# One order table for all operations, and half of the weights' low words scaled on GpSimd

## The chip, the cores and the metric

One core of a Trainium2 chip runs the whole program. The metric is the device time of one execution in microseconds (us). The engines are TensorE (PE in the profile; its weight loads are PEld), VectorE (DVE), ScalarE (ACT), GpSimd (POOL), and SyncE (SP), which issues every DMA here. The engines share nothing but memory and semaphores, and each one executes its own instructions strictly in the order in which they were emitted.

## What is computed

Random-feature attention (8 batches of 8 heads, 576 tokens, head size 64, 128 features) is followed by a two-layer network with GELU on all 4608 tokens, 512 to 2048 to 512:

```python
def phi(x):                                    # 128 features of 64 values
    proj = np.einsum('bhsd,md->bhsm', x, omega)
    h = proj - np.sum(x * x, axis=-1, keepdims=True) / 2.0
    h = h - np.max(h, axis=-1, keepdims=True)
    return np.exp(h) / np.sqrt(m)
q_p, k_p = (phi(q_s), phi(k_s))
kv, z = np.einsum('bhsm,bhsd->bhmd', k_p, v), np.sum(k_p, axis=2)
num = np.einsum('bhsm,bhmd->bhsd', q_p, kv)
den = np.einsum('bhsm,bhm->bhs', q_p, z)[..., None] + 1e-06
x = (num / den)                                # 4608 x 512
h = x @ w_in
out = (0.5 * h * (1.0 + erf(h / sqrt(2)))) @ w_out
```

The two weight matrices arrive as 64-bit words and are put together as 32-bit floats on the core.

## The kernel before

**Units.** Attention is cut into 32 units, each two heads of one batch, called u0 to u31. The units of batch 0 (u0 to u3) and of batch 1 (u4 to u7) take a plain 32-bit path (`unit_plain`, L1093 on): `pair` and `shared` project the keys and queries on PE (L951, L958), `top` finds maxima on DVE (L963), `exp_tiles` (L967) or `shift_tiles` and one large `exps` (L972, L976) follow on ACT, then `kv` (L983), `q_trans` (L1021), `q_copy` (L1025), `num_plain` (L1031), `den` (L1045), `rcp` (L1056 to L1058), `div` (L1086). The units from u8 on take a split path (`split_pre`, `split_post`), in which values are carried as a high and a low part: `x_high` on ACT (L1161) and `x_low` on GpSimd (L1170) before the projections `proj` and `proj_q` (L1178, L1200), and `k_high` on GpSimd (L717 through the helper `mul`) and `k_low` on DVE (L1271) before `kv_split` (L1282).

**Blocks.** The network runs over 13 blocks of tokens (256, 256, ten of 384, 256). Block 0 uses 32-bit weights (L1461, L1487). Blocks 1 to 8 use 16-bit high and low parts: three products for each pair of operands, `mm1` (L1466), `gelu` (L1474), `g_high` on ACT (L1478), `g_low` on DVE (L1482), `mm2` (L1490 to L1492). Blocks 9 to 12 use a scheme with seven products in place of eight (`w_prod` L1679, `w_mm2` L1777 to L1779). A block can begin when the units that hold its tokens are done.

**Weights.** Each matrix comes in eight pieces, w1.0 to w1.7 (the first matrix, `w_in`) and w0.0 to w0.7 (the second). For a piece SP loads the raw words (`w_load`, L783, a ring of two buffers), ACT scales the high words (`w_hi`, L788) and converts the low words (`w_lo`, L793), DVE shifts (`w_shift`, L796), GpSimd adds the two (`w_round`, L802), and the largest magnitude is found by ACT for the first six pieces of `w_in` (`w_abs`, L809) and by DVE for the other ten (`w_max`, L805). When all eight pieces of a matrix have been seen, a short chain (`wchain_a` to `wchain_f`) makes a scale, and `w_high` (ACT, L824) and `w_low` (DVE, L828) split the matrix into 16-bit parts.

**The order.** Every step is entered into a `Planner` as an operation with an engine, a cost in us, what it reads and writes, and the ring that its buffer comes from; there are 4920 of them. `Planner.run` (L472 on) is a list scheduler that runs when the program is built: it keeps a clock for each engine, and whenever an engine is free by the costs, it emits that one of the ready operations whose due time is the earliest. The due times come from tables (`STARTS`, `UDUE`, `OFF` for each kind of operation, `MOVES` for single operations). Nothing of this remains on the chip but the order in which each engine meets its instructions.

Of the kernel before, what the change touches and what calls it, by code (L numbers as in the profile page):

```python
# [42 lines left out]
OFF = dict(b_high=-472.0, b_low=68.87, b_sum=505.92, block_be=-596.75, block_high=154.41, block_low=-26.75,  # L43
           block_out=860.38, block_scales=1087.2, block_spread=159.81, bound_a=-4.4, bound_b=540.98, bound_c=-153.41,
           c_gelu=617.86, c_high=519.15, c_low=-947.47, c_low22=-402.54, c_sum=-84.96, chain_a=-692.49, chain_b=-304.15,
           chain_c=-174.23, chain_d=-251.9, den=-276.91, div=-78.97, exp_tiles=500.86, exps=-740.41, g_high=119.81,
           g_low=32.78, gelu=410.19, identity=-401.63, k_high=-264.32, k_low=-842.67, k_shift=268.78, kv=-450.72,
           kv_a=-401.8, kv_b=-498.62, kv_b2=137.69, kv_c=126.76, kv_d=-532.78, kv_split=83.89, kvz_plain=-357.97,
           load_dup=-500.18, load_om=-454.76, load_two=-550.8, load_v=463.08, load_vst=468.47, mm1=-402.39, mm2=439.26,
           nothing=899.66, num=38.14, num_plain=198.27, p2=-435.32, pair=134.89, proj=-15.78, proj_add=-47.53,  # L50
           proj_lo=-1088.01, proj_q=-453.69, q_back=820.26, q_blocks=-307.52, q_copy=-825.62, q_high=102.71, q_low=-58.21,
           q_max=115.0, q_max2=-738.48, q_max3=-292.57, q_max4=-375.03, q_max5=-248.0, q_max6=852.42, q_shift=29.04,
           q_trans=-350.16, rcp=-489.6, s_high=944.67, s_low=-468.09, s_sum=43.05, s_sum2=-111.06, scale_om=21.42,
           shared=-393.46, shift_tiles=-284.33, split_om=1280.88, store=-902.88, store_dma=1009.48, top=161.02, v_a=122.39,
           v_b=125.44, v_max=354.57, v_scales=208.4, v_spread=-1174.86, w_abs=1352.56, w_hi=-1126.5, w_high=423.95,
           w_lo=217.93, w_load=218.15, w_low=-223.86, w_max=-31.41, w_mm2=-9.77, w_prod=14.23, w_round=665.96,
           w_seed=603.07, w_shift=-118.27, w_snap=969.6, warm=580.57, wchain_a=297.7, wchain_b=-362.6, wchain_c=-875.34,
           wchain_d=1130.76, wchain_e=-246.9, wchain_f=881.58, x_high=-158.88, x_low=-494.15, zeros=-566.36)
# [367 lines left out]
class Planner:  # L426
# [45 lines left out]
    def run(self, lat, hop, alloc, put):  # L472
# [1442 lines left out]
```

## Time and profile before

| | |
|---|---|
| Median of 3 runs | 983.53 us (982.3 to 984.62) |
| Profiled execution: its time, its span | 982.61 us, 980.8 us |
| Granted TensorE clock, mean over the span | 0.991 of full speed |
| PE busy | 954.8 us, 97% of the span |
| PE weight loads busy | 627.2 us, 64% |
| DVE busy | 752.8 us, 77% |
| ACT busy | 763.1 us, 78% |
| POOL busy | 403.2 us, 41% |
| DMA | 71.01 MB, mean 72 GB/s |

The span reaches from the first to the last instruction; 1.8 us of the execution lie around it. A busy share is an average over stages that are unlike: weights and attention fill the first 110 us, attention and network run side by side until about 890 us, and the end is network alone. So the profile is read in stretches. Matmuls overlap, so the busy time of PE counts stretches in which it had work, and its idle time is what is left.

### The profile page before, as it was taken

To read this page: it belongs to the slowest core of one execution; us is meant where nothing else is said; L and a number is where in the kernel's file an instruction comes from. 1 tells how busy PE (TensorE), PEld (TensorE's weight loads), DVE (VectorE), ACT (ScalarE), POOL (GpSimd) and SP (SyncE) were. 2 spreads that over 40 slices of the span, in tenths; PEclk is the share of its full clock that TensorE was granted. 3 is DMA by queue.
4 is the path that set the end of the run, shared out by engine and by line. 5 is a ranking of instruction groups with operands and counts; after the bars stand their busy time and mean duration, and the time that the engine had idled before them with its cause. 6 is when DMAs were issued, how large, how long until landed. Compare 5 with 4: busy or idle time off the path is not lost.

```text
span 980.8 us, 18864 instructions
## 1 busy us (share of the span) xinstructions
PE 954.8 (97%) x6572; PEld 627.2 (64%) x6572; DVE 752.8 (77%) x2007; ACT 763.1 (78%) x1591; POOL 403.2 (41%) x612
## 2 busy tenths in 40 slices
PE   7999999989999999999999999999999999999998
PEld 6666666756555556666655666566657677677676
DVE  3789889998999887989887888989888764662222
ACT  6989778888788887988899788988788765674443
POOL 2443316775658445645552653542574102130000
PEclk7989999999999999999999999999999999999999
DMA  9875114322122123124112221221021000000000
GB/s 277 242 227 192 55 49 138 100 72 57 44 70 69 45 75 94 43 70 132 50 49 84 62 63 57 62 76 58 25 56 52 25 1 34 1 1 34 1 33 23
DMA packets 46286, 71.01 MB, mean 72 GB/s; under 512 B 13680, under 2 KB 22256, under 8 KB 46192
## 3 DMA queue, kind: packets, MB, share of 16 engines
q1 hardware_dynamic: 46192, 69.81, 24.4%
q8 instruction: 52, 0.85, 0.4%
q14 instruction: 42, 0.34, 0.1%
HBM read 60.36 MB, written 9.44 MB: 71 GB/s over the span
## 4 chain that ended last, share of the span: by engine, by line
PE 51%; DVE 10%; ACT 4%; issue 1%; POOL 0%; ACTq 0%; DVEq 0%
PE h L1466 12%; PE at L1679 6%; PE h L1679 5%; PE acc L1490 4%; PE acc L1492 4%; PE acc L1491 4%; PE acc L1778 4%; PE acc L1779 4%; PE acc L1777 4%; PE at L1040 2%; PE at L1282 1%; DVE gl L1482 1%; PE at L1178 1%; PE at L1200 1%; DVE mx L1205 1%
## 5 line engine op out<-in xcount | busy, mean ns | idle before, releaser
L1170 POOL TENSOR_TENSOR r<-xt,r 64x288 fp32r<-64x288 f32 (+2 forms) x216 | 168.8, 798 | 156.7 <-ACT r L1161 122.1
L1466 PE MATMUL h<-xh,wih 128*128 128x384 f16 (+1 forms) x512 | 163.6, 320 | 6.0 <-DVE gl L1482 5.7
L1466 PE MATMUL h<-xh,wil 128*128 128x384 f16 (+1 forms) x512 | 163.7, 320 | 0.0
L1466 PE MATMUL h<-xl,wih 128*128 128x384 f16 (+1 forms) x512 | 163.7, 320 | 0.0
L1490 PE MATMUL acc<-woh,gh 128*128 128x512 f16 x368 | 140.1, 381 | 0.0
L1492 PE MATMUL acc<-wol,gh 128*128 128x512 f16 x368 | 139.5, 379 | 0.0
L1491 PE MATMUL acc<-woh,gl 128*128 128x512 f16 x368 | 139.5, 379 | 0.0
L1466 PEld LDWEIGHTS <-wih 128*128 128x128 f16 x1024 | 97.6, 98 | 56.3 <-issue 0.9
L1161 ACT CAST r<-xt 128x256 fp32r<-128x256 f32 (+2 forms) x216 | 81.4, 407 | 14.7 <-PE at L1178 6.5
L1482 DVE SCALAR_TENSOR_TENSOR gl<-h,bs,gh 128x384 f16<-128x384 f32 (+1 forms) x128 | 75.2, 590 | 16.6 <-ACT gh L1478 15.3
L1474 ACT ACTIVATE h<-h,bs 128x384 f32<-128x384 f32 (+1 forms) x128 | 68.9, 539 | 23.1 <-PE h L1466 21.8
L1478 ACT ACTIVATE gh<-h,bs 128x384 f16<-128x384 f32 (+1 forms) x128 | 72.0, 565 | 16.3 <-PE acc L1492 13.3
L1466 PEld LDWEIGHTS <-wil 128*128 128x128 f16 x512 | 50.0, 98 | 37.8 <-issue 10.1
L1777 PE MATMUL acc<-woh,gh 128*128 128x512 f16 (+1 forms) x192 | 69.4, 362 | 0.0
L1778 PE MATMUL acc<-woh,gl 128*128 128x512 f16 (+1 forms) x192 | 69.4, 361 | 0.1
L1779 PE MATMUL acc<-wol,gh 128*128 128x512 f16 (+1 forms) x192 | 69.4, 361 | 0.0
L1679 PEld LDWEIGHTS <-w 128*128 128x128 f16 x768 | 60.1, 98 | 8.3
L1492 PEld LDWEIGHTS <-gh 128*128 128x128 f16 x368 | 36.0, 98 | 43.4
L1490 PEld LDWEIGHTS <-gh 128*128 128x128 f16 x368 | 35.8, 97 | 30.9
L1051 ACT ACTIVATE dt<-at,vsc 64x288 f32<-64x288 f32 x96 | 47.6, 496 | 7.8 <-PE at L1040 5.5
L1178 PE MATMUL at<-om,r 128*128 128x256 f32 x216 | 51.2, 330 | 2.6 <-POOL r L1170 1.9
L1491 PEld LDWEIGHTS <-gl 128*128 128x128 f16 x368 | 36.1, 98 | 27.3
(291 smaller groups left out, 2510.1 us busy)
## 6 DMA issues: line engine op xcount, KB each, us to landing
xt<-in_qT SPq DMA_DIRECT2D x56, 288.0 KB, 3.8
xt<-in_kT SPq DMA_DIRECT2D x56, 288.0 KB, 3.9
out_x<-o SPq DMA_DIRECT2D x35, 256.0 KB, 2.0
raw<-in_w_in SPq DMA_DIRECT2D x16, 512.0 KB, 6.0
raw<-in_w_out SPq DMA_DIRECT2D x16, 512.0 KB, 4.8
w<-in_v SPq DMA_DIRECT2D x24, 320.0 KB, 3.0
vt<-in_v SPq DMA_DIRECT2D x8, 320.0 KB, 4.3
out_x<-o SPq DMA_DIRECT2D x2, 128.0 KB, 1.7
```

Source lines behind the costliest of these rows:

```text
L1161: nc.scalar.copy(G['r', u, x][:, 0:b - a], xf[:, a:b])
L1170: nc.gpsimd.tensor_tensor(r, xf[D:, a:b], r, op=ALU.subtract)
L1466: nc.tensor.matmul(h[:, 0:t], w, (G['xh', n, j], G['xh', n, j], G['xl', n, j])[k][:, 0:t], start=(i == 0), stop=(i == 3 * NJ - 1))
L1478: nc.scalar.activation(G['gh', n, c][:, 0:t], G['h', n, c][:, 0:t], AF.Copy, scale=G['bs', n][:, 3:4])
L1482: nc.vector.scalar_tensor_tensor(G['gl', n, c][:, 0:t], G['h', n, c][:, 0:t], G['bs', n][:, 3:4], G['gh', n, c][:, 0:t], op0=ALU.mult, op1 ...
L1490: nc.tensor.matmul(acc, gh[:, s], woh[:, c, c0:c1], start=(c == 0), stop=False)
L1491: nc.tensor.matmul(acc, gl[:, s], woh[:, c, c0:c1], start=False, stop=False)
L1492: nc.tensor.matmul(acc, gh[:, s], wol[:, c, c0:c1], start=False, stop=(c == NF - 1))
L1679: nc.tensor.matmul(b[:, g * h:(g + 1) * h], w, x[:, kt], start=first and k == 0, stop=last and k == 6 * GP - 1, skip_group_check=True)
L1777: nc.tensor.matmul(acc, gh, woh[:, c, c0:c1], start=begin, stop=False)
L1778: nc.tensor.matmul(acc, gl, woh[:, c, c0:c1], start=False, stop=False)
L1779: nc.tensor.matmul(acc, gh, wol[:, c, c0:c1], start=False, stop=end)
```

## The change

- `Planner.run` loses the scheduler, its costs, due times and tables. In their place stands `ORDER`, a list of the 4920 operations by number; a letter behind a number says which of the PSUM rings a tile takes. `run` emits them in that order. The graph of operations is the same, so every engine has the same operations as before, but for the eight of the next point; the costs in the calls of `op` are changed here and there, and are no longer used for anything.
- For every other piece of both matrices (w1.0, w1.2, w1.4, w1.6, w0.0, w0.2, w0.4, w0.6) GpSimd converts the low words (`w_lo_p`) and not ACT.
- The scale of the 16-bit key features moves into the exponential: `exps` adds a constant (a per-partition tile `kln`) for the units on the split path, `k_high` multiplies by 1 and `k_low` is a plain subtraction in place of a multiply and subtract.
- Other switches that the diff brings (`px`, `wg`, `kl`) are set so that they change nothing.

The core of the diff, tables cut:

```diff
-KSC = 2.0 ** 15
+KSC = 2.0 ** 11
+KLN = 7.6246189861593985
...
+X = dict(plain=8, kvp=8, eb0=8, ttr=1, pair=0, amax=63, qm=1, xm=0, km=0, prelu=1, n0=9, h=2, at=3, vs=5, wr=('h', 'at'),
+         tx=4, ss=4, xh=8, gh=3, xp=0, qs=0, kl=99, wl=21845, wg=0, px=0)
+ORDER = """
+0 3 6 7 151 42 41 157 4 1 8 43 9bca 14b 2 76 15 12 16 10 152 13 17 154 153 11 18 44aba 20 155 19 49b 45 21 47 50 51 163 77
...
-    def run(self, lat, hop, alloc, put):
...
+    def run(self, alloc, put):
+        done = set()
+        for x in ORDER.split():
+            i = x.rstrip('abc')
+            o, pick = self.ops[int(i)], x[len(i):] or 'a' * 4
+            assert o.deps <= done and o.after <= done
+            for (names, k), z in zip(o.new, pick):
+                name = names if isinstance(names, str) else names['abc'.index(z)]
...
             put(o)
...
+        nc.vector.memset(kln, KLN)
...
+    def w_lo_p(pc):
+        nc.gpsimd.tensor_scalar(pc.l if pc.l is not None else raw(pc)[1], raw(pc)[1].bitcast(U32), 2.0 ** -29, 1.0, op0=ALU.mult, op1=ALU.mult)
...
         op('ACT', 1.08, w_hi, pc, w=[rk + ('hi',)], r=[rk])
-        op('ACT', 1.08, w_lo, pc, r=[rk], w=pc.lk if pc.l is not None else [rk + ('lo',)])
+        on = X['wl'] >> (i + 8 * (1 - win)) & 1
+        op('POOL' if on else 'ACT', 1.5 if on else 1.08, w_lo_p if on else w_lo, pc, r=[rk], w=pc.lk if pc.l is not None else [rk + ('lo',)])
...
-            nc.scalar.activation(u.et, u.et, AF.Exp)
+            nc.scalar.activation(u.et, u.et, AF.Exp, bias=kln if u.split else 0.0)
...
-        mul(nc.gpsimd, kk[:, 0, ts], u.et[:, ts], KSC)
+        mul(nc.gpsimd, kk[:, 0, ts], u.et[:, ts], 1.0)
...
-        nc.vector.scalar_tensor_tensor(kk[:, 1, ts], u.et[:, ts], KSC, kk[:, 0, ts], op0=ALU.mult, op1=ALU.subtract)
+        (nc.gpsimd if u.k >= X['kl'] else nc.vector).tensor_tensor(kk[:, 1, ts], u.et[:, ts], kk[:, 0, ts], op=ALU.subtract)
```

What the table says, read out engine by engine and set beside the order of before (operations of each engine that stand at the same place, the mean shift of all by number of places, the largest shift):

| engine | operations | same place | mean shift | largest |
|---|---|---|---|---|
| PE | 1597 | 493 | 1.7 | 13 |
| ACT | 1375 (1383 before) | 17 | 8.1 | 71 |
| DVE | 1261 | 204 | 3.1 | 88 |
| POOL | 521 (513 before) | 3 | 7.8 | 93 |
| SP | 150 | 77 | 1.0 | 8 |

- PE before: `warm`, `pair(u0,0)`, `pair(u1,0)`, `shared(u0)`, `shared(u1)`, `pair(u0,1)`. After: `pair(u0,0)`, `shared(u0)`, `warm`, `pair(u0,1)`, `pair(u1,0)`, `shared(u1)`. (`warm` is 22 matmuls on zeros; the first two of after are the projection of the keys of u0 and the half tiles that its two heads share.)
- SP before: both loads of u0, then `load_om`. After: `load_om` first.
- ACT before: `exp_tiles` of u0 (four tiles), twice two tiles, `w_hi(w1.0)`, `w_lo(w1.0)`. After: `exp_tiles` of the two shared tiles of u0, `w_hi(w1.0)`, then eight more tiles of u0.
- ACT ahead of `exps(u4)`: the table puts the same operations there as before, less `w_lo` of w1.0, w1.2, w1.4 and w1.6, `w_abs(w1.4)` and `bound_a(u3)`. Ahead of the first `w_high`, `w_lo(w0.0)` is missing too.
- POOL: `w_lo` of a piece stands right ahead of its own `w_round`, but for w0.0.
- The number of changes between the exponential and the GELU on ACT is 56 in both orders.

## Rows read from the trace of the kernel before

**Rows 1.** The page: busy time, share of the span and instructions of each engine.

```profile
PE 954.8 (97%) x6572; PEld 627.2 (64%) x6572; DVE 752.8 (77%) x2007; ACT 763.1 (78%) x1591; POOL 403.2 (41%) x612
```

**Rows 2.** Busy us by stretch: length, PE, PEld, DVE, ACT, POOL, granted clock, DMA share, GB/s.

```profile
0.00:24.00 24.00, 18.06 (x140) 15.29 (x140) 8.84 (x25) 16.36 (x44) 5.40 (x8) 0.79 0.95 275
24.00:48.00 24.00, 21.80 (x203) 16.52 (x201) 18.01 (x47) 23.75 (x61) 9.04 (x7) 1.00 0.88 252
48.00:72.00 24.00, 21.57 (x133) 15.01 (x129) 19.30 (x54) 21.94 (x39) 10.94 (x16) 0.86 0.72 227
72.00:96.00 24.00, 24.00 (x128) 15.72 (x127) 22.83 (x41) 22.39 (x34) 9.85 (x4) 1.00 0.55 175
...
144.00:168.00 24.00, 24.00 (x154) 15.48 (x153) 20.20 (x61) 20.35 (x50) 14.11 (x25) 1.00 0.45 141
168.00:192.00 24.00, 22.85 (x171) 16.29 (x170) 23.43 (x76) 20.99 (x58) 17.30 (x27) 1.00 0.37 98
...
336.00:360.00 24.00, 23.81 (x151) 14.75 (x150) 22.84 (x62) 19.97 (x43) 12.62 (x18) 1.00 0.21 55
...
696.00:720.00 24.00, 21.57 (x120) 12.54 (x119) 20.61 (x62) 18.97 (x46) 19.73 (x37) 1.00 0.18 50
```

**Rows 3.** Waits of PE, whole span: us in total, times, longest us.

```profile
PE h L1466 <- DVE gl L1482: 5.7, 9, 1.6
```

**Rows 4.** Timeline of ACT, 0 to 75 us: start us, duration us, what [idle before].

```profile
8.24 1.14 ACT L967 ACTIVATE et<-at,nm 128x128 f32<-128x128 f32 x4 [6.22 <-DVE nm L963]
...
12.20 1.14 ACT L793 ACTIVATE w<-raw 128x1024 int32<-128x1024 uint32 x1
13.22 1.14 ACT L967 ACTIVATE et<-h,nm 128x128 f32<-128x128 f32 x4
...
50.33 1.08 ACT L809 ACTIVATE w<-w 128x1024 f32<-128x1024 f32 x1
...
54.92 2.12 ACT L976 ACTIVATE et<-et 128x2304 f32<-128x2304 f32 x1 [0.21 <-DVE et L972]
```

**Rows 5.** Timeline of PE, 0 to 75 us.

```profile
1.05 4.88 PE L742 MATMUL h<-w 128*128 128x256 bf16 x22 [1.05 <-DVE w L733]
6.06 1.52 PE L951 MATMUL at<-om,xt 64*128 64x128 f32 x17
...
15.46 2.07 PE L951 MATMUL at<-om,xt 64*128 64x128 f32 x14 [4.76 <-ACT et L967]
...
44.93 2.28 PE L983 MATMUL acc<-vt,w 128*128 128x65 f32 x18
...
57.10 3.58 PE L983 MATMUL at<-vt,et 128*128 128x65 f32 x18 [1.15 <-ACT et L976]
```

**Rows 6.** Timeline of all engines, 0 to 30 us: first use of the feature matrix.

```profile
5.78 0.23 DVE L749 TENSOR_SCALAR om<-om 128x128 f32<-128x128 f32 x1 [4.17 <-DMA om<-in_omT]
```

**Rows 7.** POOL by line and shape, whole span: count, busy us, mean ns, idle us before.

```profile
L802 POOL TENSOR_TENSOR w<-w 128x1024 int32<-128x1024 int32 x12 | 28.7, 2391 | 47.2 <-ACT w L793 36.3 <-DVE w L796 10.8
...
L717 POOL TENSOR_SCALAR vt<-et 128x256 f16<-128x256 f32 x52 | 22.5, 449 | 49.4 <-ACT et L976 22.4 <-PE at L1282 21.1 <-ACT h L1474 5.7
```

**Rows 8.** Timelines of DVE, 100 to 120 us, and of POOL, 60 to 125 us.

```profile
101.87 0.74 DVE L828 SCALAR_TENSOR_TENSOR wil<-w,wsc,wih 128x512 f16<-128x512 f32 x1
...
111.33 2.04 DVE L828 SCALAR_TENSOR_TENSOR wil<-w,wsc,wih 128x512 f16<-128x512 f32 x1
...
110.42 2.40 POOL L802 TENSOR_TENSOR w<-w,raw 128x1024 int32<-128x1024 int32 x1 [3.80 <-ACT gh L1472]
```

**Rows 9.** DVE by line and shape, whole span, as in rows 7.

```profile
L1242 DVE TENSOR_TENSOR ql<-qt,qh 128x576 fp32r<-128x576 f32 x48 | 36.9, 774 | 2.4 <-ACT qh L1239 2.3
...
L1271 DVE SCALAR_TENSOR_TENSOR vt<-et,vt 128x256 f16<-128x256 f32 x52 | 23.2, 470 | 0.6 <-POOL vt L717 0.6
```

**Rows 10.** Timeline of DVE, 204 to 210 us.

```profile
206.11 0.78 DVE L1306 TENSOR_REDUCE vmax<-w 128x1 f32<-128x640 f32 x1
206.81 0.61 DVE L1482 SCALAR_TENSOR_TENSOR gl<-h,bs,gh 128x384 f16<-128x384 f32 x1
```

More of the change, by code (lines that the diff above doesn't have):

```diff
@@ L43 @@
[L43 to L58, printed above, removed]
@@ new lines, in run @@
+    def run(self, alloc, put):
[6 more added lines that the diff above has]
+                name = names if isinstance(names, str) else names['abc'.index(z)]
+                bufs, got = self.rings[name]
+                if len(got) >= bufs:
+                    assert all(u in done for u in self.users[got[-bufs]])
+                got.append(k)
@@ L516, in emit @@
                 alloc(name, k)
             put(o)
-            if o.e == 'SP':
-                free['SP'] = t + 0.06
-                self.dma = max(self.dma, t + 1.6) + o.size / 245e3
-                o.end = self.dma
-            elif o.e:
-                c = o.c
-                if o.e == 'PE':
-                    c = clock(t, c)
-                if o.tab and o.tab != self.tab:
-                    c += X['tsw']
-                    self.tab = o.tab
-                free[o.e], o.cc = t + c, c
-                if o.e == 'POOL' or o.e == 'DVE' and o.fn.__name__ in PORT:
-                    port[o.e] = t + c
-                o.end = t + c + lat[o.e] + (X['pm'] if o.kind is None else 0.0)
-            else:
-                o.end = t
@@ L609, in run @@
-        return max(o.end for o in self.ops)
+            done.add(o)
+        assert len(done) == len(self.ops)
 @with_exitstack
@@ L902, in weights_split @@
     def weights_split(win, c):
-        op('ACT', 0.63, w_high, win, c, r=[('w32', win, c), ('wsc', win), ('macc', win)], w=[('wh', win, c)], kind='W')
+        on = X['wg'] >> (c + 16 * (1 - win)) & 1
+        op('POOL' if on else 'ACT', 0.8 if on else 0.63, w_high_p if on else w_high, win, c, r=[('w32', win, c), ('wsc', win), ('macc', win)], w=[('wh', win, c)], kind='W')
         op('DVE', 0.67, w_low, win, c, r=[('w32', win, c), ('wsc', win), ('wh', win, c)], w=[('w', win, c)], kind='W')
@@ L1102, in out_ops @@
            new=[(ring, k) for k in pn])
-        n = 0.5 if not u.split else 0.92
+        n = 0.5 if not u.split else 1.03
         op('ACT', n, den, u, half, r=pn + ([('vsc', u.b)] if not u.kp else []), new=[('dt', ('dt', u, half))])
-        op('DVE', 0.92, rcp, u, half, r=[('dt', u, half)], new=[('rt', ('rt', u, half)), ('rc', ('rc', u, half))])
-        c = sum(0.15 + (c1 - c0) / 960 for _, c0, c1, _ in ps) * (2 if u.split else 1)
+        op('DVE', 1.165, rcp, u, half, r=[('dt', u, half)], new=[('rt', ('rt', u, half)), ('rc', ('rc', u, half))])
+        c = sum(0.17 + (c1 - c0) / 900 for _, c0, c1, _ in ps) * (2 if u.split else 1)
         op('DVE', c, div, u, half, due=(2, 2 * u.k + half, 0.0, 0.0), r=pn + [('rt', u, half)], w=keys)
@@ L1409, in split_post @@
                 op('POOL', 0.1 + 0.15 * n, k_high, u, g, r=es + ['kk'], w=[('kk', g)])
-                op('DVE', 0.1 + 0.14 * n, k_low, u, g, r=es, w=[('kk', g)])
+                if u.k >= X['kl']:
+                    op('POOL', 0.16 + 0.24 * n, k_low, u, g, r=es, w=[('kk', g)])
+                else:
+                    op('DVE', 0.1 + 0.14 * n, k_low, u, g, r=es, w=[('kk', g)])
             for g in range(len(KG)):
@@ L1870, in favor_attention_ffn @@
             op(None, 0, nothing, w=['xaf'] + [('xa', m, j) for m in range(2) for j in range(NJ)] + [('xp', k, j) for k in (4, 5) for j in range(2)])
-    lat = dict(PE=0.18, ACT=0.107, DVE=0.07, POOL=0.046)
-    hop = dict(PE=0.2, ACT=0.023, DVE=0.023, POOL=0.06)
     last = {}
```

211 lines of the change are left out of this document (69 added, 142 removed), and 520 rows, old and new, of tables (MOVES, ORDER, UDUE).

## The prediction

> **What bounds the kernel now.** I read the busy times first, then the stretches of 24 us, then PE's waits, and at last the timelines of the stretches in which PE is not full. PE is busy for 954.8 of 980.8 us [rows 1], and the work on PE is the same after the change: the graph has the same operations. So the most that an order can bring is PE's idle time, 26 us, and what PE loses at the lower of its two clock levels (1.2 against 2.4 GHz). The stretches [rows 2] say where that lies. From 0 to 72 us PE lacks 5.9, 2.2 and 2.4 us, and the granted clock is 0.79 and 0.86 in the first and the third. In the four stretches from 72 to 168 it is full. In the eight from 168 to 360 (the first and the last are shown) it lacks 8.0 us in sum, DVE being at 23.4 of 24 in the first. Then come single waits, 2.4 us of them in 696 to 720, and from 744 us on PE is full.
>
> What ends the waits differs. From 8.2 us to about 62 us ACT has hardly a gap (23.75 of 24 us busy in the second stretch [rows 2]; its only long wait is the first, 6.22 us [rows 4]). PE waits for it at 15.46 (4.76 us) and at 57.10 (1.15 us, for the large exponential of u4) [rows 5]. After 57 us PE has a backlog. So the head ends when ACT comes to `exps(u4)`, at 54.92 [rows 4]. In the middle the largest sum, 5.7 us in nine waits, is `mm1` waiting for a PSUM bank that `g_low` on DVE has to free [rows 3]: there DVE ends last.
>
> **The conversions that leave ACT.** By the table, five operations that stood ahead of `exps(u4)` no longer do: `w_lo` of w1.0, w1.2, w1.4 and w1.6, which are gone from ACT, and `w_abs(w1.4)`, which comes later. A `w_lo` lasts 1.14 us, but the next operation starts 1.02 us after it [rows 4]; the magnitude pass lasts 1.08 us [rows 4]. That is 4 x 1.02 + 1.08 = 5.2 us less work ahead of the point that ends the head. The magnitude pass only moves, but `w_lo(w0.0)` is missing ahead of the first `w_high` as well, so that there again some 5 us are saved. The other three conversions leave ACT after 72 us, where PE is full [rows 2]: nothing there.
>
> **The same work on GpSimd.** No row shows this conversion on POOL. The nearest of its kind, one input times a number, takes 449 ns for 256 columns [rows 7]; in proportion, 1024 columns are 1.8 us, less if part of the 449 ns is fixed. The two-input `w_round` of the same size takes 2.39 us [rows 7], the upper end; the lower is ACT's 1.14 us. I take 1.5, nearer to the one-input row. Eight of them are 12 us (9 to 19) on an engine that is idle for 61 of the first 96 us [rows 2]. Each stands ahead of its own `w_round` and needs only the loaded words, so it runs while ACT does `w_hi`; POOL's other work queued behind it is the small `bound_c`, for which nobody waits before the scales of block 1. Free, as long as POOL stays idle; without that cover it is 1.5 us a piece.
>
> **The new start.** Before, `warm` runs from 1.05 us while the loads are on their way, and the first projection follows at 6.06 us [rows 5]. After, the two projections stand ahead of `warm`. `warm` shows what a first matmul pays: 22 of 256 columns in 4.88 us [rows 5], 222 ns each, the 1.2 GHz level (256 columns at 2.4 GHz would be 107 ns). The first 17 matmuls of the projections took 1.52 us at full clock [rows 5]; at half, `pair(u0,0)` and `shared(u0)` together take about 4 us, so the first exponential starts near 10.3 instead of 8.24 us. ACT had by 11.2 us done 2.4 us of work; the loss is 1.5 us. Then `pair(u0,1)` waits behind `warm`, to 13 or 15 us, while ACT has 3.6 us of work in hand: another 0.4 to 2.4 us. I take 2.0 in all, bounds 0.5 (should the earlier load of the features, for which DVE waited 4.17 us [rows 6], bring something) and 3.9.
>
> The Trainium skill (TensorE: Matmul & The Clock Gate, section What's actually happening) has the array throttled by default, with activity releasing it, which speaks against this placement; the rows agree, with 222 ns a matmul at the start. By the page alone the loss would be the two projections at half speed, an estimate of 2 us, the same as the sum has.
>
> Head: -5.2 + 2.0 = -3.2 us. The lower clock of the third stretch (`kv` of u4 takes 3.58 us against 2.28 for u3 [rows 5]) follows a wait of PE for ACT that stays; I count it as staying, and keep up to -2.7 us for the range.
>
> **Does the gain last?** From 72 to 168 us PE is full, so it starts earlier and ends earlier. DVE has to keep up; it has 9.4 us idle in these four stretches [rows 2] (the first and the last are shown), more than the 3.2 us asked of it.
>
> **The order in the middle.** On PE the mean shift is 1.7 places; the order of before is kept there. A wait of 1.61 us at 207 us had `v_max`, 0.78 us, running on DVE right ahead of the `g_low` that PE needed [rows 10]; the table sets `v_max` further ahead, but a `q_blocks` in its place. So DVE's work ahead of PE's waits is much the same, within 2 us either way. Of the 8.0 + 2.4 us of idle PE I take a quarter, -2.5 us; bounds -8, and +8 if as many new waits arise as there were. Where an operation stands too early it stalls all behind it on its engine; the mean shift of 8 places on ACT and POOL is the reason for the upper bound.
>
> **Edits without a price.** `k_low` as a plain subtraction: a two-input subtraction takes 774 ns for 576 columns, the present form 470 ns for 256 [rows 9]; in proportion the new form would be 344 ns, with a fixed part up to 470. I take no change; the gain on DVE is at most 120 x 0.13 = 15 us, spread over 24 units, most of them where PE is full. The constant in `exps`, the factor in `k_high`, one more memset: the same instruction forms. Changes between the two tables of ACT: 56 in both orders.
>
> **Sum.** The profiled execution takes 982.6 us (span 980.8 and 1.8 around it), 0.9 under the median of the runs. 982.6 - 3.2 - 2.5 = 976.9; I say 977.0.
>
> **Rivals.**
>
> 1. *The middle opens too.* The new order removes most of PE's waits, and the lower clock of the third stretch: 982.6 - 3.2 - 8 - 2.7 = 968.7, or 967 with the wait at 700 us. For it: the costs in the code were moved toward what the trace shows, so the order may fit DVE better. Against: the order on DVE ahead of the waits has hardly changed.
>
> 2. *The gain is given back.* At 168 us DVE is full (0.57 us idle in that stretch [rows 2]). If DVE's 9.4 us of idle time before are waits that come back in the new order, PE reaches this point 3 us earlier and waits there 3 us longer: 982 us. This is also what comes out if the eight conversions hid behind something else anyway.
>
> 3. *Slower: DVE held up by GpSimd.* A `w_low` took 2.04 us in place of 0.74 while `w_round` ran on POOL from 110.42 to 112.82 [rows 8]. Each new conversion on POOL can do that to one DVE operation: 8 x 1.3 = 10.4 us. The four before 64 us are covered, since DVE has 4 to 15 us idle in each of these stretches; the other four fall after 72 us, 5.2 us on an engine with 1.2 us idle in that stretch [rows 2]. With a start at its upper bound (3.9): 982.6 - 5.2 + 3.9 + 5.2 = 986.5. It decides as soon as the delay on DVE is over what ACT saves, 3.2 us. Against it: POOL has its `w_round` of 2.4 us there already, and PE is full all the same.
> The Trainium skill (SBUF — State Buffer, section SBUF: two separate sides) says why: an exclusive lock on the port pair that both engines share, the loser fully blocked for the instruction. The rows agree: the `w_low` ended 0.55 us after POOL did. By that rule alone, each of the four later conversions costing DVE its full 1.5 us and DVE's idle time taking up half of it, the sum would be about 980.
>
> **How the numbers follow.** The forecast gets 0.50, rival 1 0.22, rival 2 0.14, rival 3 0.14. About 0.2% (2 us) is what a measurement of this kernel can tell from no change. Faster by over 0.2% (under 981.6): nearly all of the forecast and rival 1, 0.73; within: rival 2, 0.13; slower: 0.14. The range leaves out the slow half of rival 3 and the far end of rival 1: 967 to 985.
>
> **What would show it.** Right: `exps(u4)` on ACT starts near 51.5 us, not 54.9; its first exponential near 10; the first `mm1` of block 0 some 3 us before 64.7; ACT busy in all 8 to 10 us less; POOL busy 9 to 19 us more; the conversion near 1.5 us. The middle: idle PE in 168 to 360 us between 5 and 8 us. Wrong: `exps(u4)` not earlier (the start ate it), PE idle in 168 to 216 us grown by what the head won (rival 2), or `w_low`, `q_shift` and `block_low` on DVE longer on the mean (rival 3).

## The result and the profile after

The changed kernel takes 970.3 us (median, 969.37 to 971.69); the kernel before, run beside it, 982.9. The ratio is 0.987, with a 95% interval of 0.986 to 0.989: 12.5 us less, where the terms of the forecast add up to 5.7. The profiled execution takes 970.46 us (span 968.7), so the trace has 12.1 us of it.

The page of the changed kernel: busy time of each engine, as in [rows 1].

```profile
PE 945.4 (98%) x6572; PEld 623.6 (64%) x6572; DVE 768.5 (79%) x2008; ACT 754.1 (78%) x1583; POOL 416.9 (43%) x620
```

The busy time of PE fell by 9.4 us with the same instructions, its idle time only by 2.7 (26.0 to 23.3). So a busy PE was not a PE at full pace. ACT lost 9.0 us and POOL gained 13.7, as forecast. DVE gained 15.7 for the same work. That comes with the order: the same edits in the old order leave DVE at 752.0 us (`b_all`, below).

Stretches of the changed kernel, columns as in [rows 2]:

```profile
0.00:24.00 24.00, 15.35 (x139) 12.76 (x141) 8.64 (x26) 15.16 (x44) 7.38 (x10) 0.92 0.90 260
24.00:48.00 24.00, 23.42 (x212) 17.19 (x210) 19.28 (x49) 22.25 (x61) 10.73 (x7) 0.94 0.91 264
48.00:72.00 24.00, 20.89 (x142) 14.49 (x140) 20.97 (x52) 22.39 (x41) 16.50 (x20) 1.00 0.82 264
...
168.00:192.00 24.00, 23.67 (x176) 16.94 (x175) 22.94 (x73) 22.04 (x58) 17.45 (x22) 1.00 0.42 113
...
696.00:720.00 24.00, 22.73 (x143) 13.52 (x142) 21.92 (x55) 19.89 (x44) 15.99 (x27) 1.00 0.23 62
```

PE is busy for less of the first stretch than before (15.35 against 18.06), and at a higher clock: 0.92 for 0.79. In the second the clock is 0.94 for 1.00, in the third 1.00 for 0.86. Behind the start and up to 72 us, the trace before has two spells at the 1.2 GHz level, 13.4 to 23.7 and 57.8 to 64.7 us; the trace after has one, 20.2 to 27.0 us.

Timeline of PE, then of ACT, changed kernel (start us, duration us, idle before), which answer to [rows 4, 5]:

```profile
8.24 3.39 PE L434 MATMUL h<-w 128*128 128x256 bf16 x22
...
55.12 2.28 PE L690 MATMUL at<-vt,et 128*128 128x65 f32 x18 [2.02 <-ACT et L683]
57.24 1.04 PE L728 MATMUL at<-ident,et 128*128 128x128 f32 x8
58.20 1.19 PE L738 MATMUL acc<-w 128*64 128x288 f32 x8
59.33 2.86 PE L1171 MATMUL h<-xa,w 128*128 128x256 f32 x12
```

```profile
8.82 0.63 ACT L674 ACTIVATE et<-acc,nm 128x128 f32<-128x128 f32 x2 [6.81 <-DVE nm L670]
...
52.95 2.12 ACT L683 ACTIVATE et<-et 128x2304 f32<-128x2304 f32 x1 [1.08 <-DVE et L679]
```

`exps(u4)` starts 2.0 us earlier than before, not 3.4; the first product of block 0 starts at 59.33 us against 64.69, 5.4 us earlier. The kernel before, PE:

```profile
64.69 2.76 PE L1461 MATMUL h<-xa,w 128*128 128x256 f32 x12
```

So 3.4 us are won behind `exps(u4)`. From the start of `kv(u4)` (57.10 us before [rows 5], 55.12 after) to that product PE does the same matmuls without a wait in both traces, but for one small transpose. They take 7.6 us before, nearly all at the lower clock, and 4.2 after, at the higher.

**Where the time went.** Wall time at one place misleads, since the order of PE's work differs. So each PE operation is counted with its median share of PE's busy time over all traces of this study, and these are added up to a time: PE's work done by then. What a kernel has done more than the kernel before is its lead, in us. The leads are worked out so from the traces; the ratios are to the kernel before, run beside each, with the 95% interval. Kernels of different rounds are compared by their ratios (0.001 is 1 us). One execution of `tuned2` took 1977 us and is left out.

| Kernel | ratio to before | lead at 72 | 168 | 216 | 360 | 696 | 960 us |
|---|---|---|---|---|---|---|---|
| changed | 0.9873 (0.9858 to 0.9888) | 4.7 | 4.4 | 6.6 | 8.6 | 9.7 | 11.9 |
| `a_act` | 0.9907 (0.9894 to 0.9920) | 2.2 | 2.0 | 4.1 | 5.8 | 6.8 | 9.1 |
| `a_stt` | 0.9876 (0.9863 to 0.9889) | 4.4 | 4.2 | 6.4 | 7.9 | 9.0 | 11.2 |
| `warm_first` | 0.9869 (0.9856 to 0.9881) | 4.6 | 4.4 | 6.1 | 7.3 | 8.4 | 10.5 |
| `b_pool` | 0.9986 (0.9976 to 0.9995) | 0.3 | -0.6 | 0.1 | -0.1 | 0.3 | 0.3 |
| `b_all` | 0.9992 (0.9982 to 1.0003) | 0.9 | 0.2 | 0.9 | -0.6 | -0.3 | -0.1 |
| `head_new` | 0.9959 (0.9943 to 0.9975) | 1.1 | 0.2 | 0.5 | -1.1 | -0.9 | -0.7 |
| `head_old` | 0.9920 (0.9907 to 0.9932) | 0.5 | 0.5 | 2.6 | 4.3 | 5.1 | 7.2 |
| `pe_old` | 1.0772 (1.0758 to 1.0786) | -7.7 | -9.7 | -11.4 | -14.5 | -40.4 | -64.6 |
| `shift_first` | 1.0019 (1.0008 to 1.0031) | -2.3 | -3.1 | -2.4 | -3.4 | -3.8 | -3.6 |
| `fill_kv` | 1.0011 (0.9999 to 1.0024) | 0.0 | -0.6 | 0.0 | -0.2 | -1.0 | -0.9 |
| `head_fix` | 1.0032 (1.0020 to 1.0045) | -2.7 | -3.1 | -3.1 | -4.0 | -4.4 | -4.2 |
| `head_fix_act` | 1.0022 (1.0013 to 1.0032) | -2.8 | -4.0 | -3.3 | -2.9 | -3.2 | -3.0 |
| `head_fix2` | 1.0041 (1.0029 to 1.0054) | -2.9 | -5.6 | -5.6 | -5.2 | -5.5 | -5.4 |
| `head_fix2_act` | 1.0062 (1.0048 to 1.0075) | -2.6 | -5.0 | -5.3 | -6.4 | -7.1 | -7.0 |
| `two_moves` | 1.0004 (0.9994 to 1.0014) | 0.8 | 0.0 | 1.4 | 1.0 | 1.3 | -1.3 |
| `moves_spread` | 1.0010 (1.0001 to 1.0019) | 1.2 | 0.4 | 1.9 | 1.6 | 1.9 | -1.4 |
| `tuned` | 0.9873 (0.9860 to 0.9886) | 4.7 | 4.6 | 6.7 | 9.3 | 10.3 | 11.9 |
| `tuned2` | 0.9856 (0.9839 to 0.9873) | 4.1 | 3.9 | 6.1 | 8.3 | 9.4 | 11.6 |

So of the 11.9 us, 4.7 are won up to 72 us, nothing to 168, 4.2 from there to 360, 1.1 to 696, and 2.3 at 700 to 744.

### The profile page after: what moved, and what is told of

The parts are those of the page before. It is cut to its first block, busy times and chain, and to the rows that moved or that the text cites. A ratio compares the mean times of both kernels' runs of the same rounds, so it can differ in the third digit from the quotient of the medians.

```text
span 968.7 us, 18815 instructions
## 1 busy us (share of the span) xinstructions
PE 945.4 (98%) x6572; PEld 623.6 (64%) x6572; DVE 768.5 (79%) x2008; ACT 754.1 (78%) x1583; POOL 416.9 (43%) x620
## 4 chain that ended last, share of the span: by engine, by line
PE 80%; DVE 10%; ACT 5%; issue 2%; DMA 2%; POOL 1%; SPq 0%; ACTq 0%; POOLq 0%; DVEq 0%
PE h L1176 20%; PE acc L1200 6%; PE acc L1201 6%; PE acc L1202 6%; PE at L1389 6%; PE h L1389 5%; PE acc L1487 4%; PE acc L1488 4%; PE acc L1489 4%; PE at L747 3%; PE acc L1197 3%; PE h L1171 3%; PE at L907 2%; PE at L885 2%; PE at L989 2%
## 5 line engine op out<-in xcount | busy, mean ns | idle before, releaser
L877 POOL TENSOR_TENSOR r<-xt,r 64x256 fp32r<-64x256 f32 (+2 forms) x216 | 176.9, 829 | 187.3 <-ACT r L868 160.1
L868 ACT CAST r<-xt 128x256 fp32r<-128x256 f32 (+2 forms) x216 | 83.6, 404 | 17.1 <-PE at L907 9.8
L1184 ACT ACTIVATE h<-h,bs 128x384 f32<-128x384 f32 (+1 forms) x128 | 69.1, 539 | 15.4 <-PE h L1176 14.5
L885 PE MATMUL at<-om,r 128*128 128x256 f32 x216 | 58.3, 351 | 1.3 <-DVE mx L918 0.7
L907 PE MATMUL at<-r,om 128*128 128x288 f32 x192 | 50.7, 355 | 1.1 <-POOL w L1308 0.6
```

The lines of the kernel that those rows point to most:

```text
L868: nc.scalar.copy(G['r', u, x][:, 0:b - a], xf[:, a:b])
L877: nc.gpsimd.tensor_tensor(r, xf[D:, a:b], r, op=ALU.subtract)
L885: nc.tensor.matmul(o[:, t], r[:, t * P:(t + 1) * P], om, start=True, stop=True)
```

## The experiments

"Table" is the changed kernel's order, "old order" that of the kernel before, written out as such a table. "All edits" are the conversions on GpSimd, the new `k_low` and the new constant. In these kernels a line stands some lines further down than in the changed kernel (`exps` at L691, not L683).

### The edits one by one

`a_act` moves the conversions alone, `a_stt` the form of `k_low` alone. `b_pool` has the old order and `k_low` in its old form, with the conversions on GpSimd and also the constant in the exponential; `b_all` has all edits and the old order. No run has the constant alone.

```diff
 # a_act (table), and in both kernels named _act below
-         xp=0, qs=0, kl=99, wl=21845, wg=0, px=0)
+         xp=0, qs=0, kl=99, wl=0, wg=0, px=0)
 # a_stt (table) and b_pool (old order)
-        (nc.gpsimd if u.k >= X['kl'] else nc.vector).tensor_tensor(kk[:, 1, ts], u.et[:, ts], kk[:, 0, ts], op=ALU.subtract)
+        nc.vector.scalar_tensor_tensor(kk[:, 1, ts], u.et[:, ts], 1.0, kk[:, 0, ts], op0=ALU.mult, op1=ALU.subtract)
 # b_pool and b_all: ORDER is the order of the kernel before
```

> The changed kernel and its table of orders, but the eight conversions back on ACT, each at the place in the order where the table has it. Theory 1 (the prediction's: ACT's work ahead of the large exponential of u4 sets the head): four conversions of 1.02 us stand ahead of exps(u4) again, so it starts 4 us later than at 52.95 and the time is 970.3 + 4 = 974 to 975. Theory 2 (the order alone made the gain, the conversions hid behind something else): 970 to 971. Theory 3 (the table was fitted to the conversions' place, and puts them on ACT ahead of exponentials): over 976.

> The kernel before with its own order of all operations, k_low in its form; the eight conversions alone go to GpSimd. Theory 1 (ACT's work ahead of exps(u4) sets the head): four conversions less ahead of it, 4 us, so 982.9 - 4 = 979, with exps(u4) near 51 us instead of 54.9. Theory 2 (the order alone made the gain): 982 to 984. Theory 3 (GpSimd holds up DVE): 984 to 987.

> The kernel before with its own order, and every other edit of the change: the eight conversions on GpSimd, k_low as a plain subtraction, the constant in the exponential. What it has over the changed kernel is the price of the order alone. Theory 1 (head by the conversions, middle by the order): about the time of the run with the conversions alone, 979, plus up to 2 us for the 6.6 us more of DVE work. Theory 2 (all by the order): 983 to 985. Were the order to bring nothing, it would be 970 to 972.

> The changed kernel, k_low as before in form (input times a number, here 1.0, minus the second input; the numbers that come out are the same). In the traces the 120 plain subtractions last 59.4 us in sum against 52.8 us of the form before, so DVE gets some 6.6 us back over the whole run. Theory 1 (prediction: no price where PE is full): within 1 us of 970.3. Theory 2 (DVE ends last in the middle, each 0.1 us of it there shows): up to a third of the 6.6 us comes out as time, 968 to 969.5.

Measured: with the table, the conversions are worth 973.8 - 970.3 = 3.5 us (3.3 by the ratios). The traces have 2.8 us of it, 2.5 by 72 us (leads of 4.7 and 2.2). In the old order the same eight conversions are worth 1.0 us (1.4 by the ratios), 0.3 in the trace. Why, the trace of `b_pool` says. ACT, the start of `exps(u4)`:

```profile
54.61 2.12 ACT L691 ACTIVATE et<-et 128x2304 f32<-128x2304 f32 x1 [0.84 <-DVE et L687]
```

ACT is free 0.84 us ahead and waits for DVE. The row that says so stood in the trace of the kernel before. DVE there:

```profile
53.01 0.68 DVE L972 TENSOR_TENSOR et<-at,nm 128x512 f32<-128x512 f32 x1
53.60 0.68 DVE L796 TENSOR_SCALAR w<-raw 128x1024 int32<-128x1024 int32 x1
54.20 0.69 DVE L972 TENSOR_TENSOR et<-at,nm 128x512 f32<-128x512 f32 x1
```

The last shift of u4 ends at 54.89 us; `exps(u4)` started at 54.92 [rows 4]. Two limits ended at the same time, and only one of them was lifted.

The form of `k_low` has no measurable price either way (`a_stt` 970.75), nor does it change how long `k_low` lasts. The expectations of `b_all` and `a_stt` put 6.6 us of DVE's time down to the plain subtraction (120 of them last 59.4 us in the changed kernel, against 52.8 before). They belong to the order. DVE by line and shape, `before`, `b_all`, `a_stt` and the changed kernel:

```profile
L1271 DVE SCALAR_TENSOR_TENSOR vt<-w,vt 128x256 f16<-128x256 f32 x44 | 18.6, 451 | 1.0 <-POOL vt L717 0.9
L986 DVE TENSOR_TENSOR vt<-w,vt 128x256 f16<-128x256 f32 x44 | 18.9, 458 | 1.1 <-POOL vt L416 1.0
L986 DVE SCALAR_TENSOR_TENSOR vt<-w,vt 128x256 f16<-128x256 f32 x44 | 26.0, 605 | 0.8 <-POOL vt L416 0.8
L978 DVE TENSOR_TENSOR vt<-w,vt 128x256 f16<-128x256 f32 x44 | 26.2, 611 | 0.8 <-POOL vt L408 0.8
```

The old order gives 451 and 458 ns, the table 605 and 611, with the old and the new form each time. Of the 96 `k_low` of 256 columns, 62 run beside a pass on GpSimd in the changed kernel (615 ns on the mean) and 48 in `b_all` (520); the others take 406 and 413.

`b_all` is within 1 us of `b_pool`. What is left, 982.6 - 970.3 = 12.3 us (11.7 by the ratios), is the order, the conversions being on GpSimd in both. It includes the PSUM rings that the table names: 15 tiles, all of u0 to u3, take another ring than in the old order. No run takes the table's order and the old rings, so the head's gain is that of both.

### Head or middle, and PE's own order

`head_new` and `head_old` change from one order to the other at `mm1(0,4,1)`, near 76 us. `warm_first` is the table with the warming matmuls first on PE. `pe_old` is the table with PE's order alone taken back.

```diff
 # warm_first, order on PE
-pair(u0,0) shared(u0) warm pair(u0,1) ...
+warm pair(u0,0) shared(u0) pair(u0,1) ...
```

> All edits of the change (conversions on GpSimd among them). The order is the table's up to the product mm1(0,4,1), near 76 us, and from there on the order of the kernel before. By the work that PE has done at 72 us, the changed kernel is 4.65 us ahead of the kernel before, the old order with the same edits (982.6) 0.9 us. Theory 1 (what the head wins lasts to the end, and the rest of the gain is the order after it): 982.6 - 3.8 = 979. Theory 2 (it is given back at 168 to 216 us, where DVE is full; rival 2 of the prediction): 982 to 983. Were the whole gain of the order to come from its head: 970 to 971.

> The reverse: all edits, the old order up to mm1(0,4,1), then the table's. Theory 1 (head and middle add up): the head loses 3.8 us, so 970.3 + 3.8 = 974. Theory 2 (the middle's order is good only for a PE that comes early): over 977. Theory 3 (a PE that comes late finds more of DVE's work done, so that part of the loss comes back): 971 to 973.

> The changed kernel with the 22 warming matmuls first on PE again, as before (and the memset of their operand first on DVE). Theory 1 (the prediction: the projections behind a cold start cost 2.0 us): 968 to 969. Theory 2 (the head is bound by something that does not care when the first projections end): 970 to 971. Theory 3 (the clock, given back early, falls in a later wait, and the projection behind the wait is late): over 971.5.

> The changed kernel, PE's own order taken back to that of before (mean shift 1.6 places, 0.04 away from the old order); DVE, ACT and GpSimd keep the table's order. Theory 1 (the prediction: PE's order is kept, so what the order wins comes from the vector engines' orders): 970 to 972. Theory 2 (the few places on PE are what opens its waits, since a matmul whose input is late is put behind one whose input is there): 976 to 982.

Measured: `head_new` 979.1, `head_old` 975.6. By the ratios and from `b_all`, the new head brings 3.2 us alone and 4.6 on top of the new middle; the middle 7.1 alone and 8.5 on top of the head. Alone they add up to 10.3 of the 11.7 us that both bring; the 1.4 us between are within the intervals. So most of what the head wins lasts, and the middle's gain does not need it.

The profiled execution of `head_new` is the slowest of its six, 983.3 us at a mean clock of 0.991; the other five are 978.3 to 980.5 at 0.993 to 0.996. It is an experiment by itself: up to 76 us it has the changed kernel's order, but its granted clock is 0.57 from 56 to 64 us, where the changed kernel has 1.00. PE there:

```profile
56.25 3.96 PE L698 MATMUL at<-vt,et 128*128 128x65 f32 x18 [2.02 <-ACT et L691]
63.71 2.64 PE L1179 MATMUL h<-xa,w 128*128 128x256 f32 x11
```

From `kv(u4)` to the first product it takes 7.5 us with no wait between; the changed kernel takes 4.2. So with the new head the lower clock costs 3.3 us, and that is why the leads of `head_new` are low in the table. Why the clock fell in this execution, the runs don't show: the wait of PE ahead of `kv(u4)`, 2.02 us, is the same in both traces.

`warm_first` takes 970.7: where the warming stands makes no difference. The first projections start at 5.19 us, when their input has landed, and by 48 us the leads are the same (1.1).

`pe_old` takes 1059.5 us, 88 more than the changed kernel by the ratios, for a mean shift of 1.6 places on PE. Its page, and its longest waits of PE (us in total, times, longest):

```profile
PE 977.4 (92%) x6572; PEld 630.9 (60%) x6572; DVE 769.3 (73%) x2008; ACT 753.0 (71%) x1583; POOL 414.3 (39%) x620
```

```profile
PE h L1184 <- DVE gl L1200: 13.2, 19, 1.8
PE acc L1496 <- DVE gl L1431: 5.0, 8, 2.3
PE at L893 <- POOL r L885: 5.0, 7, 1.5
```

Against the changed kernel's page, DVE, ACT and POOL have next to nothing more to do. PE stands idle for 79.6 of 1057.0 us, in many waits; these three are the largest sums. So the orders fit one another as a whole, and a small mean shift says nothing of its worth.

### One wait at a time, in the head

All have all edits and the old order, and change its head by hand.

```diff
 # shift_first, DVE
-chain_a div(u2,0) chain_b top top shift(u4) w_shift(w1.6) shift(u4)
+div(u2,0) top top shift(u4) shift(u4) chain_a chain_b w_shift(w1.6)
 # fill_kv
+        if u.k == 4:
+            for _ in range(28):
+                nc.tensor.matmul(G['pk', u][:, 0:P], z16[:, 0:P], z16[:, 0:P], start=True, stop=True)
 # head_fix: shift_first, and ACT, PE (on DVE rcp, div of (u3,0) follow;
 # w_max(w1.6), w_shift(w1.7) and wchain_c go further back)
-exps(u4) den(u2,1) w_hi(w1.7) w_lo(w1.7) den(u3,0)
+exps(u4) den(u2,1) den(u3,0) w_hi(w1.7) w_lo(w1.7)
-num_plain(u3,1) q_trans(u4,1) wchain_b mm1(0,0,0) ... mm1(0,1,2)
+q_trans(u4,1) num_plain(u3,1) mm1(0,0,0) ... mm1(0,1,2) wchain_b
 # head_fix2: head_fix, PSUM rings as the table names them, and DVE
-div(u3,0) chain_d ... kvz_plain(u4)
+div(u3,0) kvz_plain(u4) w_shift(w1.7) chain_d w_max(w1.6) w_max(w1.7)
```

> All edits, the order of the kernel before, but on DVE the last four steps for u4 (two tops, two shifts) go ahead of chain_a, chain_b and w_shift(w1.6), 1.2 us of work. In the trace of the kernel before, the last shift of u4 ends at 54.89 us and exps(u4) starts on ACT at 54.92. Theory 1 (with the conversions off ACT the head is bound by DVE's way to that shift): exps(u4) 1.2 us earlier than in the run with the old order (53.9), 982.6 - 1.2 = 981.4. Theory 2 (ACT's queue still holds exps(u4)): no change of its start, 982 to 983.

> All edits, the order of the kernel before, and 28 matmuls of zeros (128 columns each) at the head of kv(u4), into the bank that kv(u4) overwrites. They run while PE waits for exps(u4), some 1.5 us from 54.3 us on. In the run with the old order PE idles 1.7 us there, and the granted clock is 0.5 from 56 to 63 us. Theory 1 (the lower clock follows that wait and costs its full price): the clock stays at 1.0 and 2.5 to 3.4 us are won, 979 to 980. Theory 2 (the clock falls for the sum of the waits before, or what it costs is hidden): 982 to 983, or 984 where the filling stands ahead of kv(u4).

> All edits, the order of the kernel before, with its head changed by hand around exps(u4): on DVE the tops and shifts of u4 first (as in shift_first); on ACT den(u3,0) ahead of w_hi and w_lo of w1.7; on DVE rcp and div of (u3,0), which the first product needs, right behind; on PE q_trans(u4,1) ahead of num_plain(u3,1), and wchain_b behind the first six products. Theory 1 (the head of the old order holds several ends behind one another: the shift of u4, then den, rcp and div of (u3,0), then kvz_plain and the bank; only taking away all of them brings what the table brings): mm1(0,0,0) near 59.5 us instead of 63.7, 982.6 - 3.5 = 979.1. Theory 2 (a further wait is behind these too, or PE's lower clock comes back): 981.5 to 984.

> As head_fix, with the eight conversions on ACT. Theory 1 (the conversions are worth their time on ACT as soon as nothing else holds exps(u4), as with the table's order, where they are worth 2.8 us of the traces): 2 to 3 us more than head_fix. Theory 2 (in the old order the conversions hide, as they did alone, 0.3 us of the traces): within 0.7 us of head_fix.

> As head_fix (all edits, the order of the kernel before with its head changed by hand), and two things more. The PSUM banks of num_plain(u3,0), num_plain(u3,1), q_trans(u3) and q_trans(u4) are taken from the rings that the table names, so that no matmul ahead of the first products waits for the bank that kvz_plain(u4) has to free; and on DVE kvz_plain(u4) goes directly behind div(u3,0), ahead of three passes over weights. In head_fix num_plain(u3,1) waited 3.46 us for kvz_plain(u4). Theory 1 (the bank that kvz_plain(u4) frees is the last of the waits that hide behind one another): mm1(0,0,0) near 60 us instead of 63.7, no wait for kvz, 979 to 980. Theory 2 (the next wait takes it, for instance the scales of w1 behind the passes that were put back): 981.5 or more.

> As head_fix2, with the eight conversions on ACT. Theory 1 (with the waits behind them gone the conversions show): 2 to 3 us more than head_fix2. Theory 2: within 0.7 us of it.

Measured: by the ratios all six are slower than `b_all`, by 2 to 7 us (the interval of `fill_kv` overlaps that of `b_all`). Yet each did what it was made for, and the traces show what came next. PE in `shift_first`, `fill_kv`, `head_fix` and `head_fix2`, one line each (two of `head_fix2`):

```profile
62.50 0.70 PE L736 MATMUL at<-ident,et 128*128 128x128 f32 x4 [3.02 <-DVE kvz L707]
```

```profile
62.95 0.63 PE L739 MATMUL at<-ident,et 128*128 128x128 f32 x4 [1.79 <-DVE kvz L710]
```

```profile
62.28 0.71 PE L746 MATMUL at<-w 128*64 128x288 f32 x4 [3.46 <-DVE kvz L707]
```

```profile
60.65 2.86 PE L1179 MATMUL h<-xa,w 128*128 128x256 f32 x12
...
71.43 0.58 PE L558 MATMUL at<-ct,ones 1*128 1x1 f32 x2 [5.37 <-DVE ct L555]
```

In `shift_first` `exps(u4)` starts at 52.94 instead of 53.89, as wanted; PE then stands 3.02 us before a PSUM bank that `kvz_plain(u4)` on DVE has to free. In `fill_kv` the clock holds at 1.0 from 48 to 72 us (0.84 and 0.88 in its two halves in `b_all`); PE comes to the same bank sooner and waits there: from 48 to 72 us its lead grows by 0.3 us, where that of `b_all` stays level. So the low clock cost the old order next to nothing; it ran down a wait that stood behind it. The trace of `moves_spread` (next section) shows the same by chance. Its head is the old order, untouched, and its clock held too (1.00 from 56 to 64 us, against 0.57 in `b_all`):

```profile
61.52 0.63 PE L736 MATMUL at<-ident,et 128*128 128x128 f32 x4 [1.78 <-DVE kvz L707]
63.16 0.27 PE L552 MATMUL at<-ident,wcm 128*1 128x128 f32 x1 [1.01 <-ACT qh L740]
63.27 2.75 PE L1179 MATMUL h<-xa,w 128*128 128x256 f32 x12
```

Four traces thus give the time from `kv(u4)` to the first product. In the old order it is 7.6 us at the low clock (`b_all`) and 7.4 at the high one (`moves_spread`); in the new order it is 7.5 at the low clock (`head_new`) and 4.2 at the high one (changed kernel). So the 3.4 us need both, an order without waits at this place and the clock that holds.

In `head_fix2` the bank of `kvz_plain(u4)` is out of the way and the first product starts at 60.65, not 63.69; then PE waits 5.37 us for the scale of `w_in`, whose step on DVE the hand-made order had left behind a magnitude pass of w0.0, and from 67 to 77 us the clock is at 0.50. With the conversions back on ACT, `head_fix` does not change (986.1 against 986.6) and `head_fix2` loses 2.0 us, with intervals that just overlap.

What follows: in the old order the head had several ends close behind one another. Lifting one of them brings nothing, or less than nothing. The changed kernel has no wait of PE from `kv(u4)` to the first product, so the table lifts them together, and by the ratio of `head_new` that is worth 3.2 us. Which of its moves are enough was not found. The hand-made heads brought waits of their own, so their times don't price the waits that they lifted.

### Single places in the middle

`two_moves` and `moves_spread`: all edits, old order; `tuned` and `tuned2`: the changed kernel.

```diff
 # two_moves and moves_spread, DVE, near 207 us
-k_low(u9,2) rcp(u8,1) v_max(u14) g_low(2,0)
+g_low(2,0) k_low(u9,2) rcp(u8,1) v_max(u14)
 # two_moves: b_low(9,3), (9,2), (9,1) behind div(u27,1); moves_spread: where the table has them
 # (on POOL b_sum(10,3) follows, in moves_spread b_sum(10,2) too)
 # tuned and tuned2, DVE; ACT
-q_blocks(u11,0) q_back(u10,0) g_low(2,3)
+g_low(2,3) q_blocks(u11,0) q_back(u10,0)
-store(2,2) gelu(3,0)
+gelu(3,0) store(2,2)
 # tuned alone, DVE
-q_blocks(u29,2) q_blocks(u29,3) k_low(u28,4)
+k_low(u28,4) q_blocks(u29,2) q_blocks(u29,3)
```

> All edits, the order of the kernel before, and two places of DVE's order changed as the table has them: g_low(2,0) goes ahead of k_low(u9,2), rcp(u8,1) and v_max(u14) (PE waited 1.61 us for it at 207 us), and b_low(9,3), (9,2) and (9,1), which no matmul reads before 741 us, go from 708 to 712 us behind div(u27,1) (PE waited 1.39 us at 712 us). PE's and ACT's orders are the old ones. Theory 1 (single places on DVE make the waits of the middle): PE's wait at 207 us under 0.4, and some 1.5 us less around 712 us, 982.6 - 2.7 = 980. Theory 2 (DVE is full, so what does not wait here waits at the next product): the wait at 207 us moves on by some us, 982 to 983.

> All edits, the order of the kernel before, with g_low(2,0) ahead as in two_moves, and b_low(9,3), (9,2), (9,1) on DVE each at the place where the table has it (behind kv_b(u28), q_max4(u29), q_low(u28,1), apart from one another), instead of all three behind div(u27,1), where PE then waited 2.44 us for g_low(8,9). Theory 1 (single places on DVE make the waits of the middle): the 1.5 us that the first move kept to 700 us in two_moves, plus 1.5 us around 712 us: 979.5 to 980. Theory 2 (DVE is full around 712 us, and the wait only moves): 981 to 982.

> The changed kernel with three places of its table changed: g_low(2,3) on DVE ahead of q_blocks(u11,0) and q_back(u10,0) (PE waits 1.29 us for it at 219 us), gelu(3,0) on ACT ahead of a store (1.08 us at 283 us), k_low(u28,4) on DVE ahead of two q_blocks (0.96 us at 716 us). Theory 1 (these are the waits that are left, each of one misplaced operation): 970.3 - 1.2 - 0.6 - 0.8 = 967.7. Theory 2 (DVE is full there, a wait removed comes back some us later): 969.5 to 971.

> The changed kernel with the first two of the three places of tuned (g_low(2,3) ahead, gelu(3,0) ahead of a store); the third, which brought a wait of 2.04 us at 717 us, is left out. By the trace of tuned the two are worth 0.6 us to 700 us. Theory 1: 969.7. Theory 2 (later waits take it back): 970.3 to 971.

Measured: nothing that can be told from no change. The wait of 1.6 us at 207 us goes away in `two_moves`, but two smaller ones come (0.36 and 0.48 us), and by 288 us the lead over `b_all` is zero again. (From 312 to 696 us it is 1.5. About half of that is a low clock: 0.57 from 288 to 292 us in `b_all`, 1.00 in `two_moves`, and 1.00 too in `fill_kv`, which has the order of `b_all` there. Whether the rest comes from the move was not settled.) Moving `b_low` away from 712 us takes one wait there and makes a longer one. PE, `two_moves`, then `tuned`:

```profile
720.84 0.32 PE L1184 MATMUL h<-xh,wih 128*128 128x384 f16 x1 [2.44 <-DVE gl L1200]
```

```profile
717.32 0.32 PE L1184 MATMUL h<-xh,wih 128*128 128x384 f16 x1 [2.04 <-DVE gl L1200]
```

In `moves_spread` the wait comes at 734 us, 3.19 us long. Behind both of these waits the clock falls (0.57 from 722 to 726 us and from 734 to 738), so they cost more than their length. `tuned` is 0.6 us ahead of the changed kernel from 360 to 696 us and gives it back at 717; `tuned2`, without that move, has a median of 969.9 us against 970.3, from three executions, with ratios whose intervals overlap. So a wait that is taken away by hand where DVE is full mostly moves on: the mechanism of rival 2, which the table as a whole escapes.

## Why the forecast was right in sign and too small

**The head.** Forecast 3.2 us, measured 4.7 by the leads. That the two are close is luck: the terms were wrong in opposite ways.

- The five operations that leave from ahead of `exps(u4)`, -5.2 us. This term failed. It took ACT's queue for the only end of the head. In the old order the four conversions are worth 0.3 us of the trace, since the shift of u4 on DVE ended 0.03 us before `exps(u4)` started; the row itself names DVE as the releaser [rows 4]. In the new order they are worth 2.5 us by the leads at 72 us.
- The new start, +2.0. This term failed too: `warm_first` shows 0 for the place of `warm`. The first exponential came at 8.82 us, not near 10. By the Trainium skill (TensorE: Matmul & The Clock Gate, section What's actually happening) the array starts throttled, and the trace agrees: in the changed kernel the first warming matmuls of 256 columns start 213 ns apart and the last ones 109, where 107 would be the 2.4 GHz level. What the slow start costs did not reach the end of the head.
- The lower clock from 48 to 72 us, counted as staying. It went, 1.00 for 0.86, and it is worth 3.3 us in the new order (`head_new` against the changed kernel), nothing in the old one (`fill_kv`, `moves_spread`). So this term, put at nothing in the sum, failed as well.
- What was missing: the work between `exps(u4)` and the first product (`den`, `rcp`, `div` of (u3,0), `kvz_plain(u4)` and its bank). The prediction ended the head at `exps(u4)`. The new order won 3.4 of its 5.4 us behind that point, where the waits had to go before the clock could count.

**72 to 168 us.** Nothing changes (4.7 to 4.4), as forecast.

**The middle.** Forecast 2.5 us for the rest of the run, measured 7.2: the term that was mis-sized most. Idle PE from 168 to 360 us fell from 8.0 to 5.0, at the lower end of the 5 to 8 that was said. But the lead grew by 4.2 us there, and by 2.3 at 700 to 744, where idle PE fell by 1.2 only. The step that failed stands in the first paragraph: that an order can bring no more than PE's idle time and its low clock. From 168 to 744 us idle PE fell by 4.4 us, and the busy time fell as well. Worked out as the time of each PE operation above the median of its kind, the busy time held 10.6 us of loss there before and 7.5 after, so 3.1 us of the gain. What the matmuls wait for inside their groups, the traces don't name, and which places of the table bring the middle's gain stays open. The second failure is the evidence: that PE's order is kept (1.7 places) and that the one operation ahead of a wait on DVE is much the same. `pe_old` shows what 1.6 places carry, 88 us. The shift of 8 places on ACT and POOL, the reason for the upper bound of this term, is mostly counting: with the eight conversions left out on both sides the mean shift is 2.3 and 2.5 places.

**The conversion on GpSimd.** POOL by line and shape, changed kernel:

```profile
L488 POOL TENSOR_SCALAR w<-raw 128x1024 int32<-128x1024 uint32 x6 | 7.2, 1197 | 9.9 <-DMA raw<-in_w_in 9.5
```

1.20 us, where 1.5 was taken and 1.14 to 2.39 were the bounds; free for PE, as said.

**`k_low`.** No price, as said. The side remark that the new form might gain up to 15 us on DVE has nothing behind it: in either order the two forms last the same.

**The rivals.** Rival 1 (968.7) came nearest, and with the right parts. The clock of the third stretch came back (3.3 us, where it had 2.7). Of the 8 us for the middle's waits it got 4.4 as idle PE and 3.1 inside groups. Its chance of 0.22 was too low. Rival 2 is what single repairs run into. Rival 3's time did not come, but what it describes happens here and there. Changed kernel, DVE (two `w_low`), then POOL (a conversion):

```profile
81.06 2.20 DVE L533 SCALAR_TENSOR_TENSOR wil<-w,wsc,wih 128x512 f16<-128x512 f32 x2
```

```profile
80.91 1.13 POOL L488 TENSOR_SCALAR raw<-raw 128x1024 int32<-128x1024 uint32 x1
```

Two `w_low` with GpSimd idle take 2 x 0.74 us. Within one order, the mean of the 32 `w_low` is 0.81 us with the conversions on ACT (`a_act`) and 0.84 or 0.88 with them on GpSimd (changed kernel, `a_stt`); in the old order 0.87, and 0.90 in `b_pool` and `b_all`. That is 1 to 2 us of DVE's time in sum, mostly where PE is full, and it does not show in the time.

## What to carry to other kernels

Before work taken off one engine is counted as time, read when the other inputs of the operation behind it are there; if they come within the same microsecond, the saving is nothing until they move as well, and the next two or three waits behind it belong to the sum. Before a low clock is counted as time, read what stands behind it: ahead of a wait it costs nothing, and once the wait is gone it costs time (here 3.3 us). PE's busy time is no floor when groups of matmuls take longer than they need: compare operations with the median of their kind. Compare instructions of two kernels within one order, or the order's effect is taken for that of the edit. Orders on several engines form one thing, so judge a new table as a whole, and don't expect single repairs at waits to add up.

## What the chip showed besides

The same program has times that follow its mean granted clock: `head_new` 978.3 us at 0.996, 980.5 at 0.993, 983.3 at 0.991. Where a low clock falls on a wait that would come anyway, it costs little (`fill_kv`); where none stands behind it, 3.3 us for one spell (`head_new`).

GpSimd still holds up DVE now and then. Changed kernel, DVE, then POOL:

```profile
711.56 2.33 DVE L978 TENSOR_TENSOR vt<-w,vt 128x256 f16<-128x256 f32 x1 [0.30 <-POOL vt L408]
```

```profile
711.50 2.11 POOL L903 TENSOR_TENSOR et<-et,nm 128x1152 f32<-128x1152 f32 x1
```

A subtraction that takes 0.41 us with GpSimd idle (the mean of 34) lasts 2.33 while a subtraction runs on GpSimd. The Trainium skill (SBUF — State Buffer, section SBUF: two separate sides) has the two share a port pair; this row agrees. So memory and semaphores are not all that these two engines share. With the table such pairs are more frequent, and `k_low` alone costs DVE 6.4 us more than in `b_all`. The order wins its 11.7 us in spite of it.
